# Agent attention with a maxout layer: 1024-token groups in two halves on the array's rows, in a written order

## Chip, core and metric

The kernel runs on one core of a Trainium2 chip. The metric is the device time of one execution in microseconds (us); less is better. The engines of the core are TensorE (PE, with its weight loads as PEld), VectorE (DVE), ScalarE (ACT), GpSimd (POOL) and SyncE (SP, which issues DMAs). TensorE's clock is granted at one of two levels, 1.2 or 2.4 GHz; the profile shows the granted share as 0.50 or 1.00.

## What is computed

Four batches of 12544 tokens with 128 channels, 49 agents for each batch, a hidden width of 768. In the reference's terms (float32 in and out):

```python
def sm(a, b):
    s = scale * (a @ b.transpose(0, 2, 1))
    e = np.exp(s - s.max(-1, keepdims=True))
    return e / (e.sum(-1, keepdims=True) + 1e-09)
agent_v = sm(agents, k) @ v                 # 49 x 128 for each batch
x = (sm(q, agents) @ agent_v).reshape(50176, 128)
h = np.maximum(np.maximum(x @ w1, x @ w2), x @ w3)
out = h @ w_out
```

Both kernels fold the 49 agents into the weights. With e the 49 unnormalised weights of a token, x @ w is e @ (agent_v @ w) up to a factor of the token, which is taken out at the end. And the maximum of three is built from differences, so that only two products of 49 rows are needed for each 128 hidden units, and a third, linear part goes straight to the output (agent_v @ w1 @ w_out, 49 x 128).

## The kernel before

Tokens are worked on in groups of 512 (GROUP = 4 blocks of 128, NG = 25 groups for a batch of 98 blocks; the last has 2 blocks). A list of 125 tasks runs through them: 25 tasks in which only the k and v of the first batch are read, then for each batch 25 tasks in which a group of its q is finished beside the same group of the next batch's k and v (none beside the last batch).

For k (L311 to L353): a block is transposed on TensorE, copied from PSUM (L314, L338), multiplied by the agents (L319, L340), put through the exponential (L323, L344), and multiplied by v with a column of ones (L349); the sum is added up in SBUF (L353). At a batch's end `phase_a_tail` makes the 49-row products of agent_v and the weight differences (gd32, gd21, G1o).

For q: four transposes (L263) and a copy (L265), scores for 49 agents (L266), exponential (L269), the sum over agents (L271) and its reciprocal (L275). Then for each of the six blocks of hidden units (f) two matmuls of 49 rows and 512 columns into the same PSUM bank: `issue_A` (L284), a relu in place on ScalarE (L286), then `issue_B` (L291) added on top, and a relu on VectorE to SBUF (L295). A task later `moe2_accum` multiplies the six results by w_out over 128 rows (L218) beside the linear part (L215), with the channels on PSUM's partitions; ScalarE copies that (L222), TensorE transposes it back to tokens (L229), ScalarE scales it by the reciprocal (L237), and ScalarE's queue stores it, 64 KB at a time (L240).

PSUM: four banks for the 49-row products (rA), two for transposes (tp), one for everything small (misc), one for the output (ao). Loads are issued from SP's queue, 64 KB each (L174, L181, L182), two tasks ahead; POOL casts q and k to bfloat16 (L196, L200), DVE casts v (L202). The tile framework's scheduler places the instructions of each engine, so an engine's list differs from the order of the code; an engine works its list in order.

## Time and profile before

| | |
|---|---|
| time, median of 2 runs | 1226.25 us (1224.52 to 1227.98) |
| span of the profiled execution | 1230.7 us |
| busy: PE, ACT, DVE, POOL | 1085.9, 569.2, 553.6, 127.4 us |
| matmuls and weight loads | 4331, 4392 |
| granted clock, mean of the span | 0.638 |
| DMA moved | 105.51 MB, 86 GB/s over the span |

A busy time is that in which the engine had an instruction running. Matmuls overlap in time, since the next starts before the last results of the one before have left; so the distance from start to start is what a matmul costs, and the length of a single one is when its result is there. In the rows "x4" means four instructions merged into one row, and "[0.90 <-POOL ...]" an idle time of that engine and what ended it.

### The profile page before, as it was taken

How to read it: one execution, taken by the hardware profiler on the slowest of the kernel's cores; microseconds unless marked ns; L12 is line 12 of the kernel's file. 1: busy time of each engine (PE TensorE's matmuls, PEld its weight loads, DVE VectorE, ACT ScalarE, POOL GpSimd, SP SyncE). 2: the span in 40 equal slices, each digit the busy share in tenths (PEclk: the TensorE clock that was granted, in tenths of full speed). 3: DMA queues.
4: the chain of work that ended last, by engine and by line, in shares of the span. 5: the costliest groups of instructions: out<-in, count | busy, mean ns of one | idle time of the engine just before them, and what ended most of it. 6: DMA issues, size and time to landing. Idle time of an engine off the chain costs nothing.

```text
span 1230.7 us, 15223 instructions
## 1 busy us (share of the span) xinstructions
PE 1085.9 (88%) x4331; PEld 363.2 (30%) x4392; DVE 553.6 (45%) x1248; ACT 569.2 (46%) x1298; POOL 127.4 (10%) x211
## 2 busy tenths in 40 slices
PE   3343999999999999999999999999999989898986
PEld 1221333333333333333333333333332222222222
DVE  2333454555554555454545545454544433333342
ACT  1000554555554555555554555555544444444444
POOL 2111101111111111111101011011100000000000
PEclk9999865666665666665666566666655555555555
DMA  5444333333333333333333333333211111111101
GB/s 156 132 133 138 109 107 106 112 100 102 86 101 97 88 103 103 103 103 99 93 96 93 92 95 106 101 103 91 59 48 39 34 50 37 47 39 45 29 18 35
DMA packets 227397, 105.51 MB, mean 86 GB/s; under 512 B 25260, under 2 KB 226928, under 8 KB 227312
## 3 DMA queue, kind: packets, MB, share of 16 engines
q1 hardware_dynamic: 170864, 78.82, 22.8%
q10 hardware_dynamic: 56448, 25.72, 7.1%
q8 instruction: 34, 0.56, 0.2%
q14 instruction: 51, 0.42, 0.1%
HBM read 78.74 MB, written 25.69 MB: 85 GB/s over the span
## 4 chain that ended last, share of the span: by engine, by line
PE 74%; ACT 7%; issue 5%; DMA 2%; ACTq 1%; DVE 1%; SPq 1%; POOL 0%; DVEq 0%; POOLq 0%
PE ao_ps L218 19%; PE rA_ps L291 17%; PE rA_ps L284 14%; PE tp_ps L229 4%; PE misc_ps L266 4%; ACT rA_ps L286 4%; PE ao_ps L215 4%; PE misc_ps L349 3%; PE tp_ps L263 3%; PE tp_ps L311 2%; ACT o_sb L237 1%; PE misc_ps L271 1%; ACTq L240 1%; ACT eqT L269 1%; DMA out_dram<-o_sb 1%
## 5 line engine op out<-in xcount | busy, mean ns | idle before, releaser
L295 DVE TENSOR_SCALAR r_sb<-rA_ps 128x512 bf16<-128x512 f32 x600 | 389.4, 677 | 336.3 <-PE rA_ps L291 333.6
L286 ACT ACTIVATE rA_ps<-rA_ps 128x512 f32<-128x512 f32 x600 | 317.3, 580 | 226.8 <-PE rA_ps L284 202.0
L291 PE MATMUL rA_ps<-eqT,gd 49*128 49x512 bf16 x600 | 305.0, 519 | 5.1 <-ACT o_sb L237 2.4
L218 PE MATMUL ao_ps<-r_sb,wo_bf 128*128 128x512 bf16 (+1 forms) x539 | 263.6, 604 | 11.5 <-issue 11.0
L284 PE MATMUL rA_ps<-eqT,gd 49*128 49x512 bf16 x600 | 241.6, 493 | 0.9 <-issue 0.9
L237 ACT ACTIVATE o_sb<-tp_ps,recips 128x128 f32<-128x128 bf16 x392 | 122.4, 363 | 98.3 <-PE tp_ps L229 49.6
L269 ACT ACTIVATE eqT<-misc_ps 49x512 bf16<-49x512 f32 (+1 forms) x100 | 58.2, 582 | 198.6 <-PE misc_ps L266 193.2
L196 POOL CAST q_bf<-qs 128x512 bf16<-128x512 f32 (+1 forms) x100 | 61.5, 615 | 597.6 <-PE tp_ps L263 433.3
L218 PEld LDWEIGHTS <-wo_bf 128*128 128x128 bf16 x600 | 63.3, 124 | 199.1 <-issue 198.0
L265 DVE COPY qT_sb<-tp_ps 128x512 bf16<-128x512 bf16 (+1 forms) x100 | 41.6, 416 | 159.4 <-PE tp_ps L263 159.4
L200 POOL CAST k_bf<-ks 128x512 bf16<-128x512 f32 (+1 forms) x100 | 60.5, 605 | 458.3 <-PE tp_ps L311 357.2
L229 PE MATMUL tp_ps<-ident_b,oT_sb 128*128 128x128 bf16 x392 | 63.7, 303 | 24.6 <-ACT oT_sb L222 24.2
L291 PEld LDWEIGHTS <-gd 49*128 49x128 bf16 x600 | 54.2, 102 | 102.7 <-issue 84.2
L284 PEld LDWEIGHTS <-gd 49*128 49x128 bf16 x600 | 57.1, 107 | 78.4 <-issue 63.9
L349 PE MATMUL misc_ps<-v_aug,e_k 128*49 128x129 bf16 x392 | 68.9, 285 | 11.9 <-ACT e_k L344 11.9
L222 ACT ACTIVATE oT_sb<-ao_ps 128x512 bf16<-128x512 f32 (+1 forms) x100 | 58.6, 586 | 28.9 <-PE ao_ps L218 14.4
L263 PE MATMUL tp_ps<-ident_b,q_bf 128*128 128x128 bf16 x392 | 61.1, 293 | 7.0 <-issue 6.0
L266 PE MATMUL misc_ps<-qT_sb,agT 128*49 128x512 bf16 (+1 forms) x100 | 59.8, 598 | 2.8 <-DVE qT_sb L265 2.7
L215 PE MATMUL ao_ps<-eqT,G1o 49*128 49x512 bf16 (+1 forms) x100 | 60.2, 602 | 1.1 <-ACT oT_sb L222 1.1
L229 PEld LDWEIGHTS <-oT_sb 128*128 128x128 bf16 x392 | 33.7, 127 | 85.5 <-ACT oT_sb L222 58.0
L349 PEld LDWEIGHTS <-e_k 128*49 128x49 bf16 x392 | 31.2, 125 | 83.9 <-issue 38.6
L275 DVE RECIPROCAL recips<-misc_ps 128x4 f32<-128x4 f32 (+1 forms) x100 | 17.8, 178 | 84.0 <-PE misc_ps L271 76.6
(56 smaller groups left out, 471.6 us busy)
## 6 DMA issues: line engine op xcount, KB each, us to landing
ks<-in_k_dram SPq DMA_DIRECT2D x392, 64.0 KB, 1.9
vs<-in_v_dram SPq DMA_DIRECT2D x392, 64.0 KB, 1.9
qs<-in_q_dram SPq DMA_DIRECT2D x392, 64.0 KB, 1.9
out_dram<-o_sb ACTq DMA_DIRECT2D x392, 64.0 KB, 1.6
wstage<-in_moe_w_dram SPq DMA_DIRECT2D x3, 384.0 KB, 3.0
wo_stage<-in_moe_w_out_dram SPq DMA_DIRECT2D x6, 64.0 KB, 4.0
ag_sb<-in_agents_dram SPq DMA_DIRECT2D x4, 24.5 KB
```

The lines of the kernel that those rows point to most:

```text
L215: nc.tensor.matmul(o_ps[:, :gtok], p["G1o"], p["eqT"][:, :gtok], start=True, stop=False)
L218: nc.tensor.matmul(o_ps[:, :gtok], wo_bf[:, f * P:(f + 1) * P], p["r_sbs"][f][:, :gtok], start=False, stop=(f == NF - 1))
L229: nc.tensor.transpose(tp_ps[:, j * P:(j + 1) * P], p["oT_sb"][:, j * P:(j + 1) * P], ident_b)
L237: nc.scalar.activation(o_sb, p["ot_ps"][:, j * P:(j + 1) * P], AF.Copy, scale=p["recips"][:, j:j + 1])
L263: nc.tensor.transpose(tp_q[:, j * P:(j + 1) * P], cst["q"][:, j, :], ident_b)
L266: nc.tensor.matmul(misc_ps[:A, :gtok], stB["agT"], qT_sb[:, :gtok], start=True, stop=True, skip_group_check=True)
L269: nc.scalar.activation(eqT[:, :gtok], misc_ps[:A, :gtok], AF.Exp, scale=scale)
L284: nc.tensor.matmul(rA_ps[:, :gtok], gd32[:, f * P:(f + 1) * P], eqT[:, :gtok], start=True, stop=True)
L286: nc.scalar.activation(rA_ps[:, :gtok], rA_ps[:, :gtok], AF.Relu)
L291: nc.tensor.matmul(rA_ps[:, :gtok], gd21[:, f * P:(f + 1) * P], eqT[:, :gtok], start=False, stop=True, skip_group_check=True)
L295: nc.vector.tensor_scalar(out=r_sb[:, :gtok], in0=rA_ps[:, :gtok], scalar1=0.0, scalar2=None, op0=ALU.max)
L349: nc.tensor.matmul(misc_ps[:A, 300:300 + P + 1], e_k[:, j * A:(j + 1) * A], cst["v"][:, j, :], start=(j == 0), stop=(j == gn - 1), skip_gr ...
```

## The change

A group is now 1024 tokens (GT = 8 blocks; 12 groups and one of 2 blocks for a batch). Its tokens are split in two halves: the scores of the even blocks are put on partitions 0 to 63, those of the odd blocks on 64 to 127 (`scores`: two matmuls with 64 output rows each). The weights of the batch (G) stand twice, on rows 0 to 48 and 64 to 112, so that `hidden` issues two matmuls of 49 rows, one for each half, on different rows of the array and into different banks of one two-bank PSUM tile (uv, three buffers, six banks). ScalarE's relu and VectorE's maximum then work on both banks at once, 1024 elements. Five of the six f blocks take the maximum of two separate products (`first`, `second`: each its own uv tile); the last keeps the old in-place way, with both steps on ScalarE.

The output product swaps its operands: the hidden results are the stationary side and w_out the moving one, 128 columns each (`out_hidden`, 48 matmuls for 1024 tokens), so that the results come out with tokens on partitions. The transposes back, their copies and ScalarE's scaling are gone; VectorE scales 512 columns at a time (`out_scale`). For k the product with v gives 49 columns, and the sum over tokens is a second product with a matrix of ones (`values`).

Loads and stores are 512 KB for a group, each partition with 8 tokens in a row, all from SP's queue. POOL casts q, k and v (ScalarE casts v of the first batch). One PSUM bank (m) serves all transposes, scores and small sums, one (o) the output.

The order is written by hand: each step is put down with a key (six units of key for a group), the list is sorted by key, and the scheduler is told to keep it. The output of a group runs one group later than its hidden part, its transposes and scores three units earlier, the k work of the next batch beside it.

The new code, cut to its core (nearly all of the old code is replaced):

```diff
+    H = 64
+    GT = 8
     NT = N // P
-    NF = Dff // P
-    GROUP = 4
-    GP = GROUP * P
-
-    groups = []
-    t0 = 0
-    while t0 < NT:
-        gsize = min(GROUP, NT - t0)
-        groups.append((t0, gsize))
-        t0 += gsize
-    NG = len(groups)
+    FI = NF - 1
+
...
+    def uv_tile():
+        return psum.tile([P, 2, 512], FP32, tag="uv", bufs=3, name="uv_ps")
+    def o_tile():
+        return psum.tile([P, 512], FP32, tag="o", bufs=1, name="o_ps")
+    def m_tile(dtype=FP32):
+        return psum.tile([P, 512 if dtype == FP32 else 1024], dtype, tag="m", bufs=1, name="m_ps")
+    ops = []
+    def at(key, fn):
+        ops.append((key, len(ops), fn))
...
+    def k_group(b, g):
+        n, t0 = sizes[g], starts[g] * P
+        key = 6.0 * (NG * (b - 1) + g - LEAD)
+        d = {}
+        def load():
+            for name, src in (("k", k), ("v", v)):
+                t = loads.tile([P, GT, C], FP32, tag=f"{name}_st", bufs=3, name=f"{name}_st")
+                nc.sync.dma_start(t[:, :n, :],
+                                  src[b, t0:t0 + n * P, :].rearrange("(p j) c -> p j c", j=n))
+                d[name] = t
+        def cast():
+            d["kb"] = work.tile([P, GT, C], BF16, tag="k_bf", name="k_bf")
+            nc.gpsimd.tensor_copy(out=d["kb"][:, :n, :], in_=d["k"][:, :n, :])
+            d["vb"] = work.tile([P, GT, C], BF16, tag="v_bf", bufs=3, name="v_bf")
+            if b == 0:
+                nc.scalar.activation(d["vb"][:, :n, :], d["v"][:, :n, :], AF.Copy)
+            else:
+                nc.gpsimd.tensor_copy(out=d["vb"][:, :n, :], in_=d["v"][:, :n, :])
+        def transposes():
+            t = d["kT_ps"] = m_tile(BF16)
+            for j in range(n):
+                nc.tensor.transpose(t[:, j * P:(j + 1) * P], d["kb"][:, j, :], ident)
...
+        def scores():
+            t = d["s"] = m_tile()
+            sumtile["t"] = t
+            for j in range(n):
+                nc.tensor.matmul(t[:, j * A:(j + 1) * A], d["kT"][:, j * P:(j + 1) * P], agT[:, b, :A],
+                                 start=(j == 0), stop=True, skip_group_check=True)
...
+        def values():
+            t = d["s"]
+            c = GT * A
+            for j in range(n):
+                e = d["e"][:, j * A:(j + 1) * A]
+                nc.tensor.matmul(t[:, c:c + A], d["vb"][:, j, :], e, start=False, stop=True,
+                                 skip_group_check=True)
+                nc.tensor.matmul(t[:, c + A:c + 2 * A], ones, e, start=False, stop=True,
+                                 skip_group_check=True)
...
+        at(key - 20, load)
+        at(key - 12, cast)
+        at(key - 0.6, transposes)
+        at(key - 0.1, evacuate)
+        at(key + 0.65, scores)
+        at(key + 1.35, exps)
+        at(key + 2.3, values)
+        at(key + 2.75, accumulate)
+        if g == NG - 1:
+            k_tail(b, key + 2.8)
+    def k_tail(b, key):
...
+        def product(i):
+            c0, c1 = i * 512, min((i + 1) * 512, WC)
+            t = m_tile()
+            for h in range(2):
+                c = c0 + (C if c0 >= C1O and h == 0 else 0)
+                nc.tensor.matmul(t[h * H:(h + 1) * H, :c1 - c0], d["avT"], wall[:, c:c + c1 - c0],
+                                 start=True, stop=True, skip_group_check=True)
+            if i % 2:
+                nc.vector.tensor_copy(out=G[b][:, c0:c1], in_=t[:, :c1 - c0])
+            else:
+                nc.scalar.activation(G[b][:, c0:c1], t[:, :c1 - c0], AF.Copy)
+        at(key, normalise)
+        for i in range(-(-WC // 512)):
+            at(key + 0.02 * (i + 1), lambda i=i: product(i))
+    def q_group(b, g):
+        n, t0 = sizes[g], starts[g] * P
+        nh = n // 2
+        T = nh * P
+        pairs = [range(0, min(2, nh)), range(2, nh)]
+        key = 6.0 * (NG * b + g)
+        d = {}
...
+        def scores():
+            t = d["s"] = m_tile()
+            for h in range(2):
+                nc.tensor.matmul(t[h * H:(h + 1) * H, :T], agT[:, b, :], d["qT"][:, h * T:(h + 1) * T],
+                                 start=True, stop=True, skip_group_check=True)
...
+        def hidden(f, col, start):
+            if start:
+                t = uv_tile()
+            else:
+                t = uv[f]
+            for h in range(2):
+                nc.tensor.matmul(t[:, h, :T], G[b][h * H:h * H + A, col + f * P:col + (f + 1) * P],
+                                 d["e"][h * H:h * H + A, :T], start=start, stop=True,
+                                 skip_group_check=True)
+            return t
+        def first(f):
+            uv[f] = hidden(f, C31, True)
+        def relu_first(f):
+            u = uv[f][:, :, :T]
+            if f == FI:
+                nc.scalar.activation(u, u, AF.Relu)
+            else:
+                a_sb[f] = work.tile([P, 2, 512], BF16, tag="a_sb", bufs=3, name="a_sb")
+                nc.scalar.activation(a_sb[f][:, :, :T], u, AF.Relu)
+        def second(f):
+            uv[f] = hidden(f, C21, f != FI)
+        def max_second(f):
+            r = r_sb[f] = work.tile([P, 2, 512], BF16, tag=f"r{f}", bufs=2, name=f"r{f}")
+            u = uv[f][:, :, :T]
+            if f == FI:
+                nc.scalar.activation(r[:, :, :T], u, AF.Relu)
+            else:
+                nc.vector.tensor_tensor(out=r[:, :, :T], in0=u, in1=a_sb[f][:, :, :T], op=ALU.max)
+        def out_linear(o):
+            t = d["o", o] = o_tile()
+            for i, jj in enumerate(pairs[o]):
+                nc.tensor.matmul(t[:, i * 2 * C:(i + 1) * 2 * C], d["e"][:, jj * P:(jj + 1) * P],
+                                 G[b][:, C1O:C1O + 2 * C], start=(i == 0), stop=False,
+                                 skip_group_check=True)
+        def out_hidden(o, part):
+            t = d["o", o]
+            for i, h, f in part:
+                jj = pairs[o][i]
+                c = (i * 2 + h) * C
+                nc.tensor.matmul(t[:, c:c + C], r_sb[f][:, h, jj * P:(jj + 1) * P], wo_bf[:, f, :],
+                                 start=False, stop=(f == NF - 1), skip_group_check=True)
+        def out_scale(o):
+            if o == 0:
+                d["out"] = work.tile([P, GT, C], FP32, tag="o_sb", bufs=3, name="o_sb")
+            j, m = 2 * pairs[o][0], 2 * len(pairs[o])
+            nc.vector.tensor_tensor(
+                out=d["out"][:, j:j + m, :],
+                in0=d["o", o][:, :m * C].rearrange("p (j c) -> p j c", c=C),
+                in1=d["r"][:, j:j + m].unsqueeze(2).to_broadcast([P, m, C]), op=ALU.mult)
+        def store():
+            row = b * N + t0
+            nc.sync.dma_start(out[row:row + n * P, :].rearrange("(p j) c -> p j c", j=n),
+                              d["out"][:, :n, :])
+        at(key - 20, load)
+        at(key - 12, cast)
+        at(key - 3.0, transposes)
+        at(key - 2.6, evacuate)
+        at(key - 1.75, scores)
+        at(key - 1.3, exps)
+        at(key + 2.05, sums)
+        at(key + 2.6, recips)
+        for f in range(NF):
+            at(key + f - 0.95, lambda f=f: first(f))
+            at(key + f - 0.4, lambda f=f: relu_first(f))
+            at(key + f, lambda f=f: second(f))
+            at(key + f + 0.5, lambda f=f: max_second(f))
+        e = key + 6
+        for o, linear, first_step, parts, scaled in ((0, 0.1, 0.3, 3, 2.9), (1, 4.06, 4.3, 2, 6.1)):
+            if not pairs[o]:
+                continue
+            whole = [(i, h, f) for i in range(len(pairs[o])) for h in range(2) for f in range(NF)]
+            per = -(-len(whole) // parts)
+            at(e + linear, lambda o=o: out_linear(o))
+            for i in range(parts):
+                part = whole[i * per:(i + 1) * per]
+                at(e + first_step + i, lambda o=o, part=part: out_hidden(o, part))
+            at(e + scaled, lambda o=o: out_scale(o))
+        at(e + 6.3, store)
...
+    with tc.manual_schedule():
+        for _, _, fn in sorted(ops, key=lambda o: o[:2]):
+            fn()
```

**Where instructions move.** TensorE, before, in the mixed stage, where a group's output product begins (G1o: linear weights; wo_bf: w_out; gd21: 49-row weights; rA_ps: bank of 49-row products):

```order
L215 LDWEIGHTS G1o_4021
L215 MATMUL ao_ps_4495<-eqT_4296,G1o_4021 128x512
L218 LDWEIGHTS wo_bf_104
L218 MATMUL ao_ps_4495<-r_sb_4314,wo_bf_104 128x512
L291 LDWEIGHTS gd21_4005
L291 MATMUL rA_ps_4346<-eqT_4296,gd21_4005 128x512
L218 LDWEIGHTS wo_bf_104
L218 MATMUL ao_ps_4495<-r_sb_4325,wo_bf_104 128x512
```

TensorE, of the change, at the end of a group's hidden part (uv_ps_1682: two-bank tile of the last f; uv_ps_1710: first f of the next group; o_ps: output; r0 to r5: hidden results):

```order
L337 LDWEIGHTS r5_1545
L337 MATMUL o_ps_1685<-wo_bf_91,r5_1545 128x128
L298 LDWEIGHTS G_748
L298 MATMUL uv_ps_1682<-e_q_1517,G_748 128x512
L298 LDWEIGHTS G_748
L298 MATMUL uv_ps_1682<-e_q_1517,G_748 128x512
L298 LDWEIGHTS G_748
L298 MATMUL uv_ps_1710<-e_q_1706,G_748 128x512
L298 LDWEIGHTS G_748
L298 MATMUL uv_ps_1710<-e_q_1706,G_748 128x512
L337 LDWEIGHTS r0_1387
L337 MATMUL o_ps_1685<-wo_bf_91,r0_1387 128x128
```

The 49-row products now come in pairs, one for each half, and stand between runs of output products that load the hidden results as weights, 12 in each of the two runs here; behind the second run follow eight k transposes.

VectorE, before, one task in the mixed stage:

```order
L265 COPY qT_sb_4773<-tp_ps_4768 128x512
L275 RECIPROCAL recips_4662<-misc_ps_4647 128x4
L295 TENSOR_SCALAR r_sb_4674<-rA_ps_4664 128x512
L295 TENSOR_SCALAR r_sb_4685<-rA_ps_4667 128x512
L295 TENSOR_SCALAR r_sb_4698<-rA_ps_4670 128x512
L295 TENSOR_SCALAR r_sb_4710<-rA_ps_4681 128x512
L295 TENSOR_SCALAR r_sb_4713<-rA_ps_4694 128x512
L295 TENSOR_SCALAR r_sb_4716<-rA_ps_4706 128x512
L353 TENSOR_TENSOR E_acc_4053<-misc_ps_4647,E_acc_4053 49x129
L202 CAST v_aug_4764<-vs_4631 128x4x128
L203 MEMSET v_aug_4764 128x4
L314 COPY kT_sb_4812<-tp_ps_4807 128x512
```

VectorE, of the change, one group of 1024 tokens in the mixed stage (m_ps and o_ps: the banks m and o; a_sb: relu of the first product):

```order
L290 RECIPROCAL recips_1834<-m_ps_1769 128x8
L193 TENSOR_TENSOR Eacc_815<-m_ps_1769,Eacc_815 128x98
L344 TENSOR_TENSOR o_sb_1839<-o_ps_1753,recips_1645 128x512
L265 COPY qT_1856<-m_ps_1844 128x1024
L323 TENSOR_TENSOR r3_1858<-uv_ps_1841,a_sb_1836 128x1024
L323 TENSOR_TENSOR r4_1892<-uv_ps_1862,a_sb_1860 128x1024
L164 COPY kT_1927<-m_ps_1914 128x1024
L344 TENSOR_TENSOR o_sb_1839<-o_ps_1874,recips_1645 128x512
L323 TENSOR_TENSOR r0_1954<-uv_ps_1929,a_sb_1925 128x1024
L323 TENSOR_TENSOR r1_1983<-uv_ps_1967,a_sb_1956 128x1024
L323 TENSOR_TENSOR r2_2021<-uv_ps_1987,a_sb_1985 128x1024
```

The k copy and the scaling of an output half now stand between the maxima of two groups, the accumulation and the other scaling between the third and the fourth maximum; the cast of v has left this engine.

## Rows read from the trace of the kernel before

**Rows 1.** The page, parts 1 and 2: busy time by engine, granted clock in slices.
```profile
PE 1085.9 (88%) x4331; PEld 363.2 (30%) x4392; DVE 553.6 (45%) x1248; ACT 569.2 (46%) x1298; POOL 127.4 (10%) x211
...
PEclk9999865666665666665666566666655555555555
```
**Rows 2.** Table by stretches; after PEclk the DMA engines' share and GB/s.
```profile
core 0: us, PE busy (x) PEld busy (x) DVE busy (x) ACT busy (x) POOL busy (x), PEclk, DMA share, GB/s
20.00:120.00 100.00, 37.56 (x276) 21.72 (x274) 32.73 (x103) 7.98 (x24) 15.83 (x26) 1.00 0.48 135
122.00:922.00 800.00, 772.09 (x3254) 272.84 (x3300) 403.74 (x926) 426.49 (x973) 91.58 (x150) 0.64 0.34 96
922.00:1222.00 300.00, 267.65 (x752) 63.60 (x764) 111.04 (x196) 130.29 (x290) 12.68 (x21) 0.50 0.13 37
...
708.60:711.60 3.00, 2.81 (x21) 1.21 (x21) 1.17 (x3) 2.25 (x5) 0.61 (x1) 1.00 0.52 144
```
**Rows 3.** Timeline (start, length, instruction, wait) of one k group, first stage.
```profile
62.31 0.61 POOL L200 CAST k_bf<-ks 128x512 bf16<-128x512 f32 x1 [2.88 <-DMA ks<-in_k_dram]
...
62.98 0.61 PE L336 MATMUL tp_ps<-ident_b,k_bf 128*128 128x128 bf16 x4 [0.90 <-POOL k_bf L200]
...
63.63 0.42 DVE L338 COPY kT_sb<-tp_ps 128x512 bf16<-128x512 bf16 x1 [0.40 <-PE tp_ps L336]
...
64.11 0.35 PE L340 MATMUL misc_ps<-agT,kT_sb 128*128 128x49 bf16 x4 [0.52 <-DVE kT_sb L338]
...
64.56 0.33 ACT L344 ACTIVATE e_k<-misc_ps 128x196 bf16<-128x196 f32 x1 [3.16 <-PE misc_ps L340]
...
65.67 0.28 DVE L353 TENSOR_TENSOR E_acc<-misc_ps,E_acc 49x129 f32<-49x129 f32 x1 [1.61 <-PE misc_ps L349]
```
**Rows 4.** Timeline of TensorE in a stretch at clock 1.00.
```profile
708.89 0.39 PE L263 MATMUL tp_ps<-ident_b,q_bf 128*128 128x128 bf16 x4
...
709.53 1.02 PE L284 MATMUL rA_ps<-eqT,gd 49*128 49x512 bf16 x4
...
710.61 0.39 PE L291 MATMUL rA_ps<-eqT,gd 49*128 49x512 bf16 x1
710.93 0.25 PE L319 MATMUL misc_ps<-agT,kT_sb 128*128 128x49 bf16 x3
```
**Rows 5.** Timeline of TensorE in a stretch at clock 0.50, last batch.
```profile
1102.36 1.86 PE L284 MATMUL rA_ps<-eqT,gd 49*128 49x512 bf16 x4
...
1105.12 0.61 PE L291 MATMUL rA_ps<-eqT,gd 49*128 49x512 bf16 x1
1105.66 0.61 PE L218 MATMUL ao_ps<-r_sb,wo_bf 128*128 128x512 bf16 x1
1106.20 0.61 PE L291 MATMUL rA_ps<-eqT,gd 49*128 49x512 bf16 x1
```
**Rows 6.** Timeline of TensorE ahead of the stretch of rows 4.
```profile
705.96 2.32 PE L218 MATMUL ao_ps<-r_sb,wo_bf 128*128 128x512 bf16 x5
```
**Rows 7.** Groups by line and shape: busy us, mean ns, idle before, releasers.
```profile
L295 DVE TENSOR_SCALAR r_sb<-rA_ps 128x512 bf16<-128x512 f32 x576 | 380.2, 688 | 328.4 <-PE rA_ps L291 326.0
L286 ACT ACTIVATE rA_ps<-rA_ps 128x512 f32<-128x512 f32 x576 | 309.5, 588 | 222.0 <-PE rA_ps L284 197.2 <-DMA out_dram<-o_sb 14.9 <-DVE qT_sb L265 7.1
...
L265 DVE COPY qT_sb<-tp_ps 128x512 bf16<-128x512 bf16 x96 | 40.4, 421 | 152.0 <-PE tp_ps L263 152.0
...
L275 DVE RECIPROCAL recips<-misc_ps 128x4 f32<-128x4 f32 x96 | 17.1, 178 | 75.0 <-PE misc_ps L271 69.4 <-ACT o_sb L237 4.7 <-PE rA_ps L284 0.2
...
L295 DVE TENSOR_SCALAR r_sb<-rA_ps 128x256 bf16<-128x256 f32 x24 | 9.2, 420 | 7.9 <-PE rA_ps L291 7.6
...
L286 ACT ACTIVATE rA_ps<-rA_ps 128x256 f32<-128x256 f32 x24 | 7.8, 383 | 4.8 <-PE rA_ps L284 4.8
...
L265 DVE COPY qT_sb<-tp_ps 128x256 bf16<-128x256 bf16 x4 | 1.2, 288 | 7.4 <-PE tp_ps L263 7.4
```
**Rows 8.** The same table: weight loads of the output product.
```profile
L218 PEld LDWEIGHTS <-wo_bf 128*128 128x128 bf16 x600 | 63.3, 124 | 199.1 <-issue 198.0
```

More of the change, by code (lines that the diff above doesn't have):

```diff
@@ L37 @@
     P = 128
+    NF = Dff // P
+    H = 64
+    GT = 8
     NT = N // P
-    NF = Dff // P
-    GROUP = 4
-    GP = GROUP * P
-    groups = []
-    t0 = 0
-    while t0 < NT:
-        gsize = min(GROUP, NT - t0)
-        groups.append((t0, gsize))
-        t0 += gsize
-    NG = len(groups)
+    FI = NF - 1
+    sizes = [GT] * (NT // GT) + ([NT % GT] if NT % GT else [])
+    starts = [sum(sizes[:i]) for i in range(len(sizes))]
+    NG = len(sizes)
+    assert all(n % 2 == 0 for n in sizes)
     const = ctx.enter_context(tc.tile_pool(name="const", bufs=1))
-    wpool = ctx.enter_context(tc.tile_pool(name="wpool", bufs=1))
@@ new lines, with prep @@
+    ag_bf = const.tile([A, B, C], BF16, name="ag_bf")
+    wo_bf = const.tile([P, NF, C], BF16, name="wo_bf")
+    w1_bf = const.tile([P, Dff], BF16, name="w1_bf")
+    w1T = const.tile([P, NF, P], BF16, name="w1T")
+    C21, C31, C1O = 0, Dff, 2 * Dff
+    wall = const.tile([P, 2 * Dff + 3 * C], BF16, name="wall")
+    nc.vector.memset(wall[:, C1O:], 0.0)
+    WC = 2 * Dff + 2 * C
+    def prep():
+        nc.vector.tensor_copy(out=ag_bf, in_=ag_st)
+        t = m_tile(BF16)
+        for b in range(B):
+            nc.tensor.transpose(t[:, b * H:b * H + A], ag_bf[:, b, :], ident[:A, :A])
+        for b in range(B):
+            nc.vector.tensor_copy(out=agT[:, b, :A], in_=t[:, b * H:b * H + A])
@@ new lines, in q_group, with load, cast, transposes @@
+    def q_group(b, g):
[4 more added lines that the diff above has]
+        key = 6.0 * (NG * b + g)
+        d = {}
+        uv = {}
+        a_sb = {}
+        r_sb = {}
+        def load():
+            t = d["q"] = loads.tile([P, GT, C], FP32, tag="q_st", bufs=3, name="q_st")
+            nc.sync.dma_start(t[:, :n, :], q[b, t0:t0 + n * P, :].rearrange("(p j) c -> p j c", j=n))
+        def cast():
+            d["qb"] = work.tile([P, GT, C], BF16, tag="q_bf", name="q_bf")
+            nc.gpsimd.tensor_copy(out=d["qb"][:, :n, :], in_=d["q"][:, :n, :])
+        def transposes():
+            t = d["qT_ps"] = m_tile(BF16)
+            for j in range(n):
+                jj, h = divmod(j, 2)
+                i = h * nh + jj
+                nc.tensor.transpose(t[:, i * P:(i + 1) * P], d["qb"][:, j, :], ident)
+        def evacuate():
+            d["qT"] = work.tile([P, GT * P], BF16, tag="qT", name="qT")
+            nc.vector.tensor_copy(out=d["qT"][:, :n * P], in_=d["qT_ps"][:, :n * P])
+        def scores():
[3 more added lines that the diff above has]
+                                 start=True, stop=True, skip_group_check=True)
+        def exps():
+            d["e"] = work.tile([P, 512], BF16, tag="e_q", bufs=3, name="e_q")
+            nc.scalar.activation(d["e"][:, :T], d["s"][:, :T], AF.Exp, scale=scale)
+        def sums():
+            t = d["sum"] = sumtile.pop("t", None)
+            fresh = t is None
+            if fresh:
+                t = d["sum"] = m_tile()
+            c = GT * A + 2 * A
+            for jj in range(nh):
+                nc.tensor.matmul(t[:, c + 2 * jj:c + 2 * jj + 2], d["e"][:, jj * P:(jj + 1) * P], sel,
+                                 start=(fresh and jj == 0), stop=True, skip_group_check=True)
+        def recips():
+            c = GT * A + 2 * A
+            d["r"] = work.tile([P, GT], FP32, tag="recips", bufs=3, name="recips")
+            nc.vector.reciprocal(d["r"][:, :n], d["sum"][:, c:c + n])
+        def hidden(f, col, start):
[24 more added lines that the diff above has]
+                nc.scalar.activation(r[:, :, :T], u, AF.Relu)
+            else:
+                nc.vector.tensor_tensor(out=r[:, :, :T], in0=u, in1=a_sb[f][:, :, :T], op=ALU.max)
[32 more added lines that the diff above has]
+        at(key + 2.6, recips)
+        for f in range(NF):
+            at(key + f - 0.95, lambda f=f: first(f))
[14 more added lines that the diff above has]
+        at(e + 6.3, store)
@@ L381 @@
+    at(-6.0 * (NG + LEAD) - 21, prep)
+    at(-6.0 * (NG + LEAD) + 12, prep_weights)
+    for b in range(B):
+        for g in range(NG):
+            k_group(b, g)
+            q_group(b, g)
+    with tc.manual_schedule():
+        for _, _, fn in sorted(ops, key=lambda o: o[:2]):
+            fn()
 _INS = ['q', 'k', 'v', 'agents', 'moe_w1', 'moe_w2', 'moe_w3', 'moe_w_out']
```

346 lines of the change are left out of this document (60 added, 286 removed).

## The prediction

> **What bounds the kernel now.** I read the page first. TensorE is busy 88% of the span and the next engine 46%, so TensorE is the bound, and its granted clock falls from 0.9 to 0.5 and 0.6 once the q work begins [rows 1]. Then the table by stage [rows 2]: in the k-only stage (20 to 120 us) TensorE is busy 38 of 100 us; in the mixed stage (122 to 922 us) 772 of 800 us at a mean clock of 0.64; in the last batch (922 to 1222 us) 268 of 300 us at 0.50. So 1100 us, or 22.4 us for each 1024 tokens, are set by TensorE, mostly at the lower of its two levels. The 1.00 of the first stage is not borne out: its four transposes took 0.61 us [rows 3], against 0.39 us where the clock was really high [rows 4].
>
> Then the timeline, for what a step costs at each level. High: four 49-row matmuls of 512 columns take 1.02 us, one 0.39, so 0.21 from start to start [rows 4]. Low: 1.86 and 0.61, so 0.42 [rows 5]. Where 49-row and 128-row matmuls alternate, starts lie 0.54 apart at the low level, and a change between the two costs 0.11; at the high level the next start after a 49-row matmul comes 0.32 later, again 0.11 more [rows 4, 5].
>
> What moves the clock: the stretch at 1.00 from 708.6 us [rows 2] came right behind five back-to-back matmuls over all 128 rows [rows 6]. In the last batch, where these alternate with 49-row ones [rows 5], it never rose, though TensorE was busy all the time [rows 2].
>
> **The change, by its prices.** Per 1024 tokens, low level then high.
>
> TensorE. The twelve hidden products stay, but each now works on both halves: rows 0-63 and 64-127 at once, 98 live rows. No row shows a pair side by side. It costs 0.42 if the halves overlap and 0.84 if they queue (half that at the high level). I take 0.42: one such pair reads the 512 columns and nearly the rows of one 128-row matmul, whose share of the alternation is that [rows 5]. The Trainium skill (TensorEngine Tiling, Tiling Modes) says that tiles work independently, loads and matmuls in parallel; by it the pair is one matmul too and the sum stays as it is below; no run here shows it.
> So: 12 pairs 5.0 / 2.5. Output: 48 matmuls of 128 columns at 0.107 / 0.06 (four take 0.61 and 0.39 [rows 3, 4]) 5.1 / 2.9, and four of 256 columns 0.9 / 0.4. The eight output transposes are gone; 16 for q and k cost 1.7 / 1.0. Scores of q 0.4 / 0.2. Scores and values of k are 24 matmuls of 49 columns at 0.05 (four in 0.35 [rows 3]) / 0.03 [rows 4]: 1.2 / 0.7. The listing has 16 changes of row grouping: 1.8 / 1.8. Sum 16.2 / 9.6 us, against 22.4 now.
>
> VectorE. 256 more elements cost 0.268 us in L295, so the two-bank max is 0.688 + 0.536 = 1.22 us, five of them 6.1; two copies of 1024 are 0.69 each; two scalings 0.69 each (L295's price); reciprocal 0.18, accumulation at most 0.28 [rows 3, 7]. Sum 9.3. ScalarE: two-bank relu 0.588 + 0.410 = 1.00, seven of them, and two exponentials, 0.59 (as L286) and 0.49 (0.33 for 196 columns and 196 more at that slope) [rows 3, 7]: 8.1. GpSimd casts v beside q and k: half more than 127 us [rows 1], under 200 us in all, and stands a group and a half ahead of need. Stores move from ScalarE's queue to SP's, where a store waits for its scaling; behind it stand loads that are issued more than three groups ahead of use, and a group's 2.1 MB take 7.5 us at 281 GB/s (135 at a share of 0.48 [rows 2]), so I price this at nothing; without that lead each store's wait would hold up a load.
>
> **The new order's chain.** Neither sum is the group's time, since every engine takes its list in order and the scratch bank m and the output bank o have one buffer each. I follow the listing round, from the accumulation to the next, with 0.05 to 0.1 us for each hand-over (copy ends 64.05, scores start 64.11 [rows 3]).
> (a) q transposes 0.06 + 0.11 + 0.86 (high 0.48), the next pair's result 0.11 + 0.61 (0.39), its relu 1.00 and two hand-overs: 2.9 / 2.3.
> (b) TensorE in a row: pair, linear part, q scores, 12 output products, two pairs, 12 more, k transposes and 0.18 drain: 6.3 / 3.7.
> (c) On VectorE the k copy and the scaling, which both stand ahead of the next max: 0.05 + 0.69 + 0.69 = 1.4.
> (d) Linear part of the other bank, 8 output products, k scores, one pair's result: 1.5 high. (e) The max: 1.27. (f) Next pair, 8 output products, 16 value products: 1.5 high. At the low level TensorE's own queue is longer than (d) to (f): 6.8.
> (g) Reciprocal and accumulation: 0.5.
> A group takes 17.8 us at the low level and 12.2 at the high one. So the gain is not bounded by VectorE's 9.3: it waits about 2 us in (b) with nothing ahead of it but the k copy.
> In the last batch the k steps drop out (0.86 + 0.69 + 0.40 + 0.80 + 0.28 low; 0.48 + 0.69 + 0.24 + 0.48 + 0.28 high): 14.8 / 10.0.
>
> **Which clock.** Hidden pairs light 98 rows where 49 were lit, and the output products follow in runs of 8 and 12 over 128 rows, like the stretch ahead of the rise [rows 6]; against that, at the high level the chain leaves TensorE idle some 2.6 of 12.2 us and transposes stand in each group. I take six tenths of the time at the high level (the mixed stage's 0.64 mean is three tenths [rows 2]). Then a group is 1/(0.6/12.2 + 0.4/17.8) = 13.9 us, in the last batch 11.5.
>
> **The rest.** The k-only stage: with one bank m a group's chain is serial: transposes 1.04, copy 0.69, scores 0.55, exponential 0.49, values 0.98, accumulation 0.28 and hand-overs 0.44 [rows 3, 7] = 4.5 us, 12.25 groups 55 us. Its 1.05 MB take 3.7 us at 281 GB/s, hidden. Now the stage waits for loads (2.88 us [rows 3]), issued in eight pieces of 64 KB; two of 512 KB replace them. To it come 10 us of start (an estimate; work is under way by the 20 us where rows 2 begin), the weights 3, the first product of agents and weights 5.4 (four times matmul 0.42 + 0.18, copy 0.6, hand-over 0.15), the first k group of the next batch 4.5 and the first q chain 3.2: 81 us. Four small groups, between 3 us (their predecessor's 48 products at the high level) and 8: 6 each, 24. Three later products of agents and weights, on VectorE's and TensorE's lists where others wait: 16. End, output of the last group and its store: 6.
> 36 x 13.9 + 12 x 11.5 + 81 + 24 + 16 + 6 = 502 + 138 + 127 = 767 us, against a profiled span of 1230.7, which is 0.4% above the runs' median of 1226.25, so I correct nothing.
>
> **The rivals.**
> Clock always high: 439 + 120 + 123 = 682 us. For it: TensorE hardly pauses. Against it: the last batch, busy 89% at 0.50 [rows 2]. The Trainium skill (TensorE: Matmul & The Clock Gate, Why this matters for your kernels) says that a TensorE kept busy without gaps runs at the full clock; by that rule this case would hold, and the trace of before disagrees, with 0.50 at 268 busy of 300 us.
> Clock always low, as in the last batch: 641 + 178 + 135 = 954.
> The halves queue, so the change doesn't do what it says: eight pairs on the chain cost 0.42 more, 3.4 us, and density stays as it was: 21.2 and 18.2 us, 763 + 218 + 140 = 1121.
> VectorE alone bounds (hand-overs hidden better than I walk them): 9.3 and 8.3 us, 335 + 100 + 122 = 557.
> The other side: weight loads come into the open. The group has 122 instead of 90 loads and most matmuls are too short to hide one; at 0.124 us each [rows 8] they add 15.1 to 16.2 = 31.3 us, 28 without k: 1127 + 336 + 130 = 1593. It decides from a group of 22.9 us on (1100 / 48). Against it: four transposes with four loads took 0.61 [rows 3].
>
> **How the numbers follow.** Forecast 0.45; always high 0.25; always low 0.16; halves queue 0.07; VectorE bound 0.04; loads exposed 0.03. Range 660 to 960 us, which leaves out the last three, 0.14, and takes in both bounds of the clock; the forecast's own range is 720 to 830. Within 2% of 1226, about what a measurement can tell from no change, only a queue of halves with some exposed loads would fall: 0.02. Slower 0.03, faster 0.95.
>
> **What would show it.** In the profile after: pairs of hidden matmuls starting almost together and 0.42 or 0.21 from pair to pair (right), or twice that; runs of output products 0.107 or 0.06 apart; VectorE's two-bank max near 1.22 us and an idle gap ahead of the k copy, ended by TensorE; k groups 4.5 us apart in the first stage; the q work from about 81 us; a granted clock between 0.7 and 0.9. A clock at 1.00 or 0.50 throughout, or VectorE without that gap, would make the forecast wrong.

## The result, and the profile after

The changed kernel takes 684.04 us (median of 2 runs, 681.0 to 687.07) against 1226.25: a ratio of 0.557, with a 95% interval of 0.551 to 0.564. The range of 660 to 960 us holds it; the point, 767, is 83 us too high. What came is close to the rival that gave 682 us, the clock always high.

Parts 1 and 2 of the page after (busy time by engine; granted clock in 40 slices), to be read beside [rows 1]:

```profile
PE 524.7 (77%) x6104; PEld 324.2 (48%) x6104; DVE 446.0 (66%) x603; ACT 416.8 (61%) x493; POOL 140.3 (21%) x149
...
PEclk9999999999999699999999699999999699999999
```

TensorE is still the busiest engine, but with 77% where it had 88%. The three dips of the clock are the three changes of batch. The table by stretches (columns as in [rows 2]):

```profile
90.00:250.00 160.00, 130.19 (x1546) 79.33 (x1543) 112.51 (x153) 102.32 (x122) 39.02 (x40) 0.97 0.43 154
250.00:480.00 230.00, 187.29 (x2308) 116.00 (x2307) 165.96 (x217) 154.10 (x180) 58.44 (x59) 0.98 0.47 169
520.00:670.00 150.00, 126.60 (x1274) 73.88 (x1273) 108.95 (x136) 103.78 (x121) 11.86 (x12) 0.95 0.24 84
...
222.70:232.90 10.20, 8.52 (x58) 4.54 (x55) 4.18 (x6) 4.39 (x7) 1.56 (x2) 0.50 0.00 0
```

The mixed stage runs at 0.98 where [rows 2] had 0.64, the last batch at 0.95 where it had 0.50. The timeline (start, length, instruction, wait) shows where the clock first rose, and one group of the mixed stage:

```profile
98.72 1.06 PE L337 MATMUL o_ps<-wo_bf,r 128*128 128x128 bf16 x8
99.97 0.39 PE L298 MATMUL uv_ps<-e_q,G 49*128 49x512 bf16 x2
...
300.82 0.61 PE L298 MATMUL uv_ps<-e_q,G 49*128 49x512 bf16 x4
301.32 2.43 DVE L323 TENSOR_TENSOR r<-uv_ps,a_sb 128x1024 bf16<-128x1024 f32 x2 [0.40 <-PE uv_ps L298]
306.51 0.39 PE L298 MATMUL uv_ps<-e_q,G 49*128 49x512 bf16 x2 [0.90 <-ACT a_sb L312]
307.50 0.84 PE L337 MATMUL o_ps<-wo_bf,r 128*128 128x128 bf16 x12
310.20 0.69 DVE L164 COPY kT<-m_ps 128x1024 bf16<-128x1024 bf16 x1 [2.14 <-PE m_ps L160]
310.81 0.68 DVE L344 TENSOR_TENSOR o_sb<-o_ps,recips 128x512 f32<-128x512 f32 x1
311.55 0.39 PE L328 MATMUL o_ps<-G,e_q 128*128 128x256 bf16 x2 [0.84 <-DVE o_sb L344]
```

Until 98 us matmuls take the times of the low level. The first run of eight output products over 128 rows (1.06 us) is followed by a pair that takes 0.39, the time of the high level. At 300.82 two pairs, four matmuls, take 0.61 us: a pair costs 0.22 and the halves overlap. VectorE waits 2.14 us ahead of the k copy, the scaling stands behind that copy, and TensorE waits another 0.84 us for the scaling.

How long a group takes, read from the reciprocals (mixed stage, then last batch) and from the k copies of the first stage:

```profile
280.57 0.21 DVE L290 RECIPROCAL recips<-m_ps 128x8 f32<-128x8 f32 x1 [0.24 <-PE m_ps L184]
292.28 0.21 DVE L290 RECIPROCAL recips<-m_ps 128x8 f32<-128x8 f32 x1 [0.24 <-PE m_ps L184]
...
602.67 0.20 DVE L290 RECIPROCAL recips<-m_ps 128x8 f32<-128x8 f32 x1
612.76 0.20 DVE L290 RECIPROCAL recips<-m_ps 128x8 f32<-128x8 f32 x1
...
52.27 0.69 DVE L164 COPY kT<-m_ps 128x1024 bf16<-128x1024 bf16 x1 [1.10 <-PE m_ps L160]
56.46 0.69 DVE L164 COPY kT<-m_ps 128x1024 bf16<-128x1024 bf16 x1 [1.10 <-PE m_ps L160]
```

That is 11.70 us, 10.08 us and 4.19 us.

### The profile page after: what moved, and what is told of

Its sections match the earlier page's. It is cut to its first block, busy times and chain, and to the rows that moved or that the text cites. A ratio compares the mean times of both kernels' runs of the same rounds, so it can differ in the third digit from the quotient of the medians.

```text
span 679.2 us, 14666 instructions
## 1 busy us (share of the span) xinstructions
PE 524.7 (77%) x6104; PEld 324.2 (48%) x6104; DVE 446.0 (66%) x603; ACT 416.8 (61%) x493; POOL 140.3 (21%) x149
## 4 chain that ended last, share of the span: by engine, by line
PE 56%; DVE 17%; ACT 10%; issue 6%; DVEq 0%; POOL 0%; ACTq 0%
PE o_ps L337 19%; PE uv_ps L298 17%; ACT a_sb L312 8%; DVE r L323 7%; PE o_ps L328 5%; DVE o_sb L344 5%; PE m_ps L261 5%; PE m_ps L160 3%; PE m_ps L270 2%; DVE kT L164 2%; DVE recips L290 1%; PE m_ps L182 1%; PE m_ps L225 1%; PE m_ps L184 1%; PE m_ps L170 1%
## 5 line engine op out<-in xcount | busy, mean ns | idle before, releaser
L312 ACT ACTIVATE a_sb<-uv_ps 128x1024 bf16<-128x1024 f32 (+1 forms) x260 | 251.3, 974 | 113.1 <-PE uv_ps L298 110.3
L323 DVE TENSOR_TENSOR r<-uv_ps,a_sb 128x1024 bf16<-128x1024 f32 (+1 forms) x260 | 295.0, 1157 | 26.5 <-PE uv_ps L298 17.8
L298 PE MATMUL uv_ps<-e_q,G 49*128 49x512 bf16 (+1 forms) x1248 | 212.8, 383 | 54.3 <-ACT a_sb L312 44.1
L337 PE MATMUL o_ps<-wo_bf,r 128*128 128x128 bf16 x2352 | 179.1, 224 | 0.0
L337 PEld LDWEIGHTS <-r 128*128 128x128 bf16 x2352 | 140.5, 100 | 53.4 <-issue 50.8
L298 PEld LDWEIGHTS <-G 49*128 49x128 bf16 x1248 | 60.1, 94 | 119.8 <-issue 84.0
L254 POOL CAST q_bf<-q_st 128x1024 bf16<-128x1024 f32 (+1 forms) x52 | 51.6, 993 | 299.7 <-issue 174.7
L150 POOL CAST k_bf<-k_st 128x1024 bf16<-128x1024 f32 (+1 forms) x52 | 51.6, 992 | 203.8 <-PE m_ps L160 186.6
L344 DVE TENSOR_TENSOR o_sb<-o_ps,recips 128x512 f32<-128x512 f32 (+1 forms) x100 | 66.7, 667 | 27.4 <-PE o_ps L337 27.4
L321 ACT ACTIVATE r<-uv_ps 128x1024 bf16<-128x1024 f32 (+1 forms) x52 | 50.7, 975 | 17.9 <-PE uv_ps L298 17.8
```

The lines of the kernel that those rows point to most:

```text
L150: nc.gpsimd.tensor_copy(out=d["kb"][:, :n, :], in_=d["k"][:, :n, :])
L254: nc.gpsimd.tensor_copy(out=d["qb"][:, :n, :], in_=d["q"][:, :n, :])
L298: nc.tensor.matmul(t[:, h, :T], G[b][h * H:h * H + A, col + f * P:col + (f + 1) * P], d["e"][h * H:h * H + A, :T], start=start, stop=True, ...
L312: nc.scalar.activation(a_sb[f][:, :, :T], u, AF.Relu)
L321: nc.scalar.activation(r[:, :, :T], u, AF.Relu)
L323: nc.vector.tensor_tensor(out=r[:, :, :T], in0=u, in1=a_sb[f][:, :, :T], op=ALU.max)
```

## The experiments

The theory to test: the number of rows that a matmul lights decides whether the clock stays high, and the clock is most of the gain. The rivals: the clock follows TensorE's busy time, or something else that the change brought. The kernels ran in three sets on three chips, each set beside runs of the kernel before (medians 1221 to 1228 us, single runs 1189 to 1236). The changed kernel itself, run once more in one of the sets:

> The changed kernel once more, on the chip and beside the runs of the next ones: 675 to 692 us, a granted clock of about 0.97, 11.70 us a group.

Measured 686.44 us (684.95 to 694.69), clock 0.96, 11.70 us a group. Differences below are against this, also where the set was another.

**Both halves on the same rows.**

```diff
-  G[b][h * H:h * H + A, ...], d["e"][h * H:h * H + A, :T]
+  G[b][0:A, ...],             d["e"][0:A, :T]
```

> The changed kernel, except that both matmuls of a hidden pair take rows 0 to 48 (the second half's hidden values are thus computed from the first half's tokens, so the odd blocks of the output are wrong). Instructions, shapes and order stay; the two halves must queue on the same rows. Theory (the rows that are lit set the clock, and the side-by-side pair gives the price of 0.22 us): a pair costs 0.42 us at the high level and 0.84 at the low one, 49 rows are lit at a time for twice as long as 98 were, and the granted clock of the mixed stage falls from 0.97 to between 0.5 and 0.75; a group takes 15 to 21 us, the whole 820 to 1120 us. Rival (the clock follows only whether TensorE is busy without gaps): TensorE is busier than before, the clock stays at 0.97, a group takes 11.7 plus eight pairs of the chain at 0.21 more, 13.4 us, the whole about 765 us.

Measured 1066.24 us, the median of 1032, 1036, 1096 and 1135; the trace is that of the run of 1096. The order on TensorE, VectorE and ScalarE is the same as in the changed kernel, instruction by instruction. Its table by stretches, and its timeline at either level:

```profile
190.00:262.00 72.00, 66.52 (x682) 36.55 (x680) 48.56 (x63) 43.21 (x50) 14.44 (x17) 1.00 0.45 160
266.00:470.00 204.00, 196.70 (x1135) 98.70 (x1134) 81.84 (x112) 74.77 (x89) 29.70 (x30) 0.50 0.28 98
...
183.94 1.88 PE L298 MATMUL uv_ps<-e_q,G 49*128 49x512 bf16 x4
190.43 1.03 PE L298 MATMUL uv_ps<-e_q,G 49*128 49x512 bf16 x4
...
133.17 0.21 DVE L290 RECIPROCAL recips<-m_ps 128x8 f32<-128x8 f32 x1 [1.50 <-PE m_ps L184]
154.85 0.21 DVE L290 RECIPROCAL recips<-m_ps 128x8 f32<-128x8 f32 x1 [1.50 <-PE m_ps L184]
...
207.40 0.21 DVE L290 RECIPROCAL recips<-m_ps 128x8 f32<-128x8 f32 x1 [0.39 <-PE m_ps L184]
220.54 0.21 DVE L290 RECIPROCAL recips<-m_ps 128x8 f32<-128x8 f32 x1 [0.38 <-PE m_ps L184]
```

Four matmuls on the same rows take 1.03 us at the high level where the pairs side by side took 0.61. The kernel has both kinds of group: 13.14 us at the high level, near the rival's 13.4, and 21.68 at the low one; the theory's 15 to 21 us lies between them, though its time held in three of the four runs. Until 188 us groups took the time of the low level, from 188 to 263 us the clock was high, then for most of the rest low, with TensorE busy 197 of 204 us and, from 286 us on, no pause longer than 0.85 us in that stretch. By the rule of the Trainium skill (TensorE: Matmul & The Clock Gate, Why this matters for your kernels) a TensorE without pauses runs at the full clock; this run disagrees, with 0.50 at 96% busy. Busy time as the cause falls.

**Queued, but on all rows.**

```diff
-  nc.tensor.matmul(t[:, h, :T], G[b][h*H:h*H+A, cols], d["e"][h*H:h*H+A, :T], ...)
+  nc.tensor.matmul(t[:, h, :T], GZ[b][h][:, cols], d["e"][:, :T], ...)   # GZ: zeros on the other half's rows
```

> The changed kernel with hidden pairs that queue but light all rows: the weights of a batch stand in two tiles, one with zeros on rows 64 to 127, the other with zeros on rows 0 to 63, and each hidden matmul runs over all 128 rows of the exponentials. The result is the same. Both theories: a pair costs 0.42 us at the high level, the clock stays at about 0.97, a group takes about 13.4 us, the whole about 765 us (740 to 790). Against the kernel in which both matmuls take rows 0 to 48 only the lit rows differ: by the theory of lit rows that one is 60 us or more slower than this one, by the rival the two are the same within 15 us. If this one is no slower than 690 us, pairs do not overlap in the changed kernel either.

Measured 710.79 us (710.70 to 711.49), clock 0.98, 12.30 us a group. The timeline of TensorE:

```profile
301.11 0.24 PE L292 MATMUL m_ps<-sel,e_q 128*128 128x2 bf16 x4
301.35 0.59 PE L306 MATMUL uv_ps<-e_q,gz 128*128 128x512 bf16 x2
301.77 0.61 PE L345 MATMUL o_ps<-wo_bf,r 128*128 128x128 bf16 x8
...
303.75 1.03 PE L306 MATMUL uv_ps<-e_q,gz 128*128 128x512 bf16 x4
305.46 0.59 PE L306 MATMUL uv_ps<-e_q,gz 128*128 128x512 bf16 x2 [0.68 <-ACT a_sb L320]
...
310.79 0.39 PE L336 MATMUL o_ps<-G,e_q 128*128 128x256 bf16 x2 [0.52 <-DVE o_sb L352]
```

The pairs queue (1.03 for four, as on the same rows), and the clock stays. In the loop only the rows differ from the run before this one, and the time differs by 355 us, by 320 at least (the fastest of one, 1031.86, against the slowest of the other, 711.49): the rows decide, and it does not matter that they carry zeros. With the rows the changes of row grouping go too, but these are not the cause: the changed kernel has 16 of them in a group and runs at 0.98.

The time is under the expected 740 to 790 us, for the group is only 0.60 us longer than the changed kernel's, not 1.7. Twelve queued pairs cost 12 x 0.21 = 2.5 us more on TensorE. Of the missing 1.9 us about 0.5 are shorter pauses of TensorE (0.68 and 0.52 us here, 0.90 and 0.84 in the changed kernel). The other 1.4 us are the 16 changes of row grouping, which are gone (at 301.77 the next products start as the pair's columns end). 1.4/16 is 0.09 us each, against the 0.11 of [rows 4, 5]. Side by side saves 24 us in all; it is not where the gain is.

**The kernel before, padded.**

```diff
-  eqT = work.tile([A, GP], ...);   gd21, gd32, G1o likewise with A rows
+  eqT = eq_z[i % 3]                # 128 rows, zeroed once; rows 0 to 48 are written as before
+  gd21, gd32 = gd_z[b % 2]         # likewise
```

> The kernel before, with the exponentials of q and the two kinds of weights of a batch padded with rows of zeros from 49 to 128, so that the hidden products and the linear part of the output light 128 rows; nothing else changes, neither count, shape of the results nor order. Theory (lit rows set the clock): the granted clock of the last batch rises from 0.50 to above 0.9 and that of the mixed stage from 0.64 likewise; TensorE's work per 512 tokens falls from 11 to about 6 us, ScalarE and VectorE have 5.8 and 5.6, the whole takes 750 to 900 us. Rival (the changed kernel's clock comes from something else that it brought, such as output products in runs of 8 and 12, fewer transposes or two tiles at once): the clock stays at 0.5 to 0.65 and the time at 1200 to 1240 us. Padding that helps only in part: 900 to 1150 us.

Measured 878.02 us (873.34 to 879.99). TensorE, ScalarE and VectorE have the same order as before, apart from the zeroing at the start. The page, the table by stretches and the timeline:

```profile
PEclk9999999999999999999999999999999999999998
...
310.00:630.00 320.00, 295.04 (x1883) 136.84 (x1913) 232.92 (x532) 244.10 (x566) 53.44 (x87) 1.00 0.50 142
650.00:860.00 210.00, 170.65 (x889) 71.32 (x900) 117.73 (x237) 146.81 (x331) 15.52 (x26) 0.94 0.21 61
...
204.23 1.04 PE L288 MATMUL rA_ps<-eq_z,gd_z 128*128 128x512 bf16 x4
...
201.52 1.05 ACTq L244 DMA_DIRECT2D out_dram<-o_sb  x2
202.62 0.63 ACT L241 ACTIVATE o_sb<-tp_ps,recips 128x128 f32<-128x128 bf16 x2 [0.87 <-ACT o_sb L241]
```

Zeros in unused rows, and nothing else, bring the old kernel from 1221 to 878 us: the clock goes from 0.64 and 0.50 to 1.00 and 0.94. That is 343 us, about six tenths of what the change gained; the fastest run of before, 1188.86 us, is still 309 us above the slowest padded one. Not all of it need be the clock. The matmul records show some 1250 changes between 49 and 128 rows before and some 210 here, and at about 0.1 us each the difference is some 100 us of TensorE's time, an estimate. How much of that is in the 343 us was not taken apart. The four hidden matmuls that took 1.86 us in [rows 5] take 1.04. Now ScalarE holds things up as well: it issues the stores itself, and each pair of issues keeps its scalings waiting (0.87 us).

**The transfers alone, with and without the padding.**

```diff
-  for j in range(gn): nc.sync.dma_start(qs[:, j, :], ...)            # k, v likewise
+  nc.sync.dma_start(qs[:, :gn, :], q[bq, rows, :].rearrange("(j p) c -> p j c", p=P))
-  for j in range(gn): ...; nc.scalar.dma_start(out[row:row + P, :], o_sb)
+  nc.sync.dma_start(out[row:row + gn * P, :].rearrange(...), o_sb[:, :gn, :])
```

> The kernel before with the padding to 128 rows, and with the transfers of the change: one load of 256 KB for each of q, k and v of a 512-token group, and one store of 256 KB from SP's queue, instead of four of 64 KB each and stores issued by ScalarE. It tells how much of what lies between the padded kernel (878 us) and the changed one (686) is the transfers. Theory (at the high clock ScalarE and the loads bound the padded kernel: ScalarE's instructions are 5.6 us per 512 tokens, its four store issues some 1.5 more, together the 7.16 us of the trace): 6.0 to 6.6 us per 512 tokens, the k-only stage about 90 instead of 105 us, the whole 710 to 790 us. Rival (the padded kernel waits for its own chain of relu, product and max, as written in its order): 7.0 us per 512 tokens, only the first stage gains, 845 to 870 us.

Measured 770.95 us (770.62 to 773.75), within the theory's range, but not by the theory: the mixed stage went from 7.16 to 7.32 us per 512 tokens, as the rival said. The gain is in the first stage (the first reciprocals come at 66.6 instead of 124 us) and in the last batch (5.8 instead of 8.0 us per 512 tokens). The scheduler that orders the kernel before also put its instructions in another order, so this run is not the transfers alone.

> The kernel before with those transfers and without the padding, so that the clock stays as it was. Theory (TensorE at the low level bounds before, the transfers are hidden behind it outside the k-only stage): the mixed stage and the last batch stay at 22 us for 1024 tokens, the k-only stage gains 10 to 30 us, 1185 to 1225 us. Rival (the transfers cost time in every stage): under 1150 us.

Measured 1051.45 us (1027.91 to 1064.96), under 1150 as the rival said, but not shown to be for its reason. The table by stretches:

```profile
20.00:100.00 80.00, 64.96 (x409) 32.11 (x408) 45.01 (x138) 26.67 (x66) 20.62 (x33) 0.95 0.80 212
...
600.00:700.00 100.00, 95.11 (x495) 32.75 (x494) 60.34 (x138) 62.25 (x144) 17.34 (x23) 0.84 0.40 116
...
800.00:1040.00 240.00, 235.56 (x849) 67.73 (x846) 120.39 (x222) 141.82 (x319) 13.95 (x23) 0.65 0.17 51
```

The first stage gained some 58 us, more than the 10 to 30 expected. The rest goes with a higher clock, 0.72 over the span instead of 0.64. Here too the scheduler changed the order on TensorE, with fewer long runs of output products (5 runs of five or six where the kernel before has 67); why this order has the high level more often is open.

The last two kernels test the padding a second time. The order on TensorE and on ScalarE is the same in both, and with the zeros the time falls from 1051 to 771 us (254 us at least, 1027.91 against 773.75) and the clock rises from 0.72 to 0.99.

**Small loads in the changed kernel.**

```diff
-  nc.sync.dma_start(t[:, :n, :], s)
+  for j in range(n): nc.sync.dma_start(t[:, j, :], s[:, j, :])
```

> The changed kernel with its loads of k, v and q cut into pieces of 64 KB, eight for one of 512 KB, as in the kernel before; stores stay. Theory (the size of the loads matters where little else is to do: the kernel before took 8.2 us for 1024 tokens of k and v in its first stage, in 16 pieces, 0.51 us each): the first stage's group goes from 4.19 to about 8 us, 45 us in all; in the mixed stage 24 pieces and a store take about 12.5 us on the queue against 11.7, another 0 to 30 us: 725 to 760 us. Rival (issuing is hidden by the lead of three groups, and the first stage of before was slow for another reason): 682 to 700 us.

Measured 757.32 us (755.70 to 758.43): 71 us lost. Timeline of the first stage (SPq is the queue that issues):

```profile
62.20 3.70 SPq L146 DMA_DIRECT2D v_st<-in_v_dram  x8
64.12 1.04 POOL L151 CAST k_bf<-k_st 128x1024 bf16<-128x1024 f32 x1 [6.68 <-DMA v_st<-in_v_dram]
66.00 3.70 SPq L146 DMA_DIRECT2D k_st<-in_k_dram  x8
```

Issuing eight pieces takes 3.7 us, so k and v of a group take 7.6 instead of 4.19 us, and the first reciprocals of q come 43 us later. In the mixed stage about half of the groups still take 11.70 us; others are longer (17.82 and 14.54 us, for two), and in the first of these GpSimd's casts wait 2.6 to 4.3 us each for loads. The mixed stage and the last batch have the other 28 us. Part of these may be the clock, 0.94 here against 0.96.

**One-bank relu and max.**

```diff
-  nc.vector.tensor_tensor(out=r[:, :, :T], in0=u, in1=a_sb[f][:, :, :T], op=ALU.max)
+  for h in range(2): nc.vector.tensor_tensor(out=r[:, h, :T], in0=uv[f][:, h, :T], ...)   # relu likewise
```

> The changed kernel with each two-bank relu and two-bank max issued as two one-bank instructions (512 elements, as in the kernel before: 0.588 and 0.688 us each). Work: five max at 1.38 instead of 1.22 us and seven relus at 1.18 instead of 1.02, 0.8 us more on VectorE and 1.1 us on ScalarE in a group. Theory (these lie on the chain that sets the group): 12.2 to 13.2 us a group, the whole 705 to 755 us. Rival (the one-bank pieces overlap TensorE better than the long ones, or both engines have the time to spare): 11.5 to 12 us, 675 to 695 us.

Measured 700.18 us (698.89 to 702.25), 12.02 us a group: 14 us, under the theory's range and above the rival's. VectorE's timeline:

```profile
300.12 2.47 DVE L327 TENSOR_TENSOR r<-uv_ps,a_sb 128x512 bf16<-128x512 f32 x4
```

and of the changed kernel:

```profile
305.72 2.35 DVE L323 TENSOR_TENSOR r<-uv_ps,a_sb 128x1024 bf16<-128x1024 f32 x2
```

Four one-bank max take 2.47 us, 0.60 from one start to the next, though a single one lasts 0.68. So two of them cost 1.20 us, not 1.38. A two-bank max lasts 1.22 us, but the next starts after 1.13 here (2.35 less 1.22), and after 1.20 in the pair at 301.32. The expectation added lengths where starts count.

**The order on VectorE and TensorE.** In the profile after, two things look wasteful: the scaling behind the k copy, and the q transposes ahead of a pair whose relu TensorE then waits for.

```diff
 k_first:      at(key - 0.6, transposes)  -> at(key - 0.72, transposes)      # k
 scale_first:  (1, 4.06, 4.3, 2, 6.1)     -> (1, 4.06, 4.3, 2, 5.85)
 q_later:      scale_first, and at(key - 3.0, transposes) -> at(key - 2.93, transposes)   # q
```

> The changed kernel with the eight k transposes ahead of the last run of 12 output products on TensorE (key -0.72 instead of -0.6). Theory (the k copy, for which VectorE waits 2.1 us a group, and the scaling behind it set the group): the k copy runs while TensorE does the 12 products and the scaling starts as these end, 0.5 us earlier than now, so a group takes 11.1 to 11.3 us and the whole 657 to 667 us, a little more than with the scaling ahead of the copy (655), since the scaling comes 0.48 us later than there. Rival (the order of these two on VectorE is all that counts): 11.7 us a group, 679 to 687 us.

> The changed kernel with the second scaling of a group put ahead of the k copy on VectorE (key 5.85 instead of 6.1). Theory: in a group the k copy waits 2.1 us for TensorE, the scaling's inputs are there before, so its 0.68 us fit into that gap, and the linear part of the output no longer waits 0.84 us for it (32.1 us in all): 11.7 falls to 10.9 to 11.3 us a group, the whole to 650 to 670 us. Rival (the wait for the scaling covers another one that ends as late, the max or the relu of the next hidden pair): less than 5 us gained, 679 to 687 us.

> The changed kernel with the scaling ahead of the k copy, and also the eight q transposes behind the next hidden pair instead of ahead of it on TensorE (key -2.93 instead of -3.0). Theory (in a group of 10.79 us TensorE's one long wait, 0.90 us, is for the relu of that pair, which stands behind the transposes and their 0.54 us): the relu starts 0.54 us earlier, the transposes fill the wait, the q copy comes some 0.3 us later on VectorE, which has 1.7 us to spare: 10.25 to 10.5 us a group, 628 to 643 us. Rival (the q copy, now later, holds up the two max behind it and with them the next pairs): 10.8 us or more, 653 to 665 us.

Measured 663.52 us (663.39 to 668.35), 655.36 us (652.46 to 659.32) and 613.29 us (611.76 to 613.55), or 11.09, 10.79 and 9.88 us a group. The first two times are as expected; the third gained more. Timelines of scale_first, then of q_later:

```profile
303.10 0.39 PE L298 MATMUL uv_ps<-e_q,G 49*128 49x512 bf16 x2 [0.90 <-ACT a_sb L312]
306.35 0.69 DVE L344 TENSOR_TENSOR o_sb<-o_ps,recips 128x512 f32<-128x512 f32 x1 [1.70 <-PE o_ps L337]
306.96 0.68 DVE L164 COPY kT<-m_ps 128x1024 bf16<-128x1024 bf16 x1
307.23 0.39 PE L328 MATMUL o_ps<-G,e_q 128*128 128x256 bf16 x2
```

```profile
303.13 0.61 PE L261 MATMUL m_ps<-ident,q_bf 128*128 128x128 bf16 x8
303.67 0.39 PE L298 MATMUL uv_ps<-e_q,G 49*128 49x512 bf16 x2
304.27 0.39 PE L298 MATMUL uv_ps<-e_q,G 49*128 49x512 bf16 x2 [0.21 <-ACT a_sb L312]
```

With the scaling first, the linear part (307.23) no longer waits. With the transposes behind the pair, the wait for the relu falls from 0.90 to 0.21 us. A wait of about 0.2 us that the transposes had for the accumulation is gone too; the two make up nearly all of the 0.91 us. This version beats both kernels, at half the time of before (ratio 0.501, 0.497 to 0.505).

## Why the prediction was right, and where its number was not

**What bounds before: right.** TensorE at the low level; the padded kernel shows it, with the same work in the same order.

**What moves the clock: right as to the rows, not as to the runs.** The prediction read from [rows 4 to 6] that runs over all 128 rows go ahead of a rise. After, the clock rises behind such a run (98.72 us), and the two kernels that differ only in rows stand 355 us apart. But the runs by themselves do not decide: with both halves on the same rows, two runs of 12 stand in every group, and the clock still stayed low for most of the time; and the kernel before with large transfers has fewer long runs and a higher clock.

**Which clock: the step that failed.** The prediction took six tenths of the time at the high level; the mixed stage had 0.98 and the last batch 0.95. It counted TensorE's pauses and the transposes against the clock. Neither did harm: TensorE pauses as foreseen (130 of 160 us busy), and the clock falls only at the changes of batch or right behind them. With this step at "always high" its own sum is 682 us, the measured time within 0.4%. That the fit is so close is luck in part: in this sum the 36 groups are 18 us too long and the rest, 123 us, is 14 us too short (137, see below). The argument was there, 98 lit rows where 49 were, and the prediction gave the case that follows from it a chance of only 0.25.

**The prices: right.** Pair 0.42 at the low level and 0.21 at the high one (measured 0.22 at the high one, queued 0.43), products 0.06 apart (12 in 0.84), changes of row grouping 0.11 (0.09), and as lengths max 1.22 (1.22), relu 1.00 (1.02), copy and scaling 0.69 (0.69 and 0.68). That the halves overlap was open, with 1121 us as the price of the other answer. It is shown now, and the Trainium skill (TensorEngine Tiling (Array Packing), Tiling Modes: tiles work independently) agrees with it. But that price took the clock to stay as in before. Queued on the same rows the kernel took 1066 us, near that price, because the clock fell with it. At the high clock, queued on all rows, it costs 24 us.

**The chain: right in size.** 12.2 us predicted, 11.70 measured; last batch 10.0 and 10.08; the gap of about 2 us ahead of the k copy is 2.14. The changes of order show that this chain, not an engine's sum, set the group: two of them together take 1.8 us from it without removing an instruction, until it is near TensorE's own 9.6 us (9.88).

**The rest: near.** The k group 4.5 (4.19), the first q work at 81 us (80.81). A change of batch with its small group took 10 to 16 us over the regular groups, where 11.3 was predicted. In all 137 us instead of 127 (679.2 less 36 x 11.70 and 12 x 10.08). That large loads matter in the first stage was right; that loads elsewhere are free fits the 512 KB loads, not those of 64 KB (28 us).

**Where the 540 us come from.** 343 come with the padding: the clock, and with it the changes of row grouping that are gone. From the padded kernel to the padded one with large transfers it is another 107, with a new order in it. The remaining 85 or so hold the overlap of the halves (24, by its removal) and the two-bank instructions (14); what is left, the token-major output and the fixed order, was not taken apart.
